# In TensorE's pinned order, which of two ready steps goes first ahead of a change of PSUM banks

## The chip, the core and the metric

The kernel runs on one core of a Trainium2 chip. The metric is the device time of one execution in microseconds. Three runs of the kernel before took 911.75, 911.88 and 913.54 us; the median is 911.88.

## The reference

Agent attention is followed by a two-layer network with a silu between. There are 2 batches of 12480 rows of 128 numbers, 49 agents, and 2048 hidden units. The input q, k and agents are drawn eight times larger than in the first lines of the reference's set-up.

```python
def sm(a, b):
    s = scale * (a @ b.transpose(0, 2, 1))
    s = s - s.max(-1, keepdims=True)
    e = np.exp(s)
    return e / (e.sum(-1, keepdims=True) + 1e-09)
a2k = sm(agents, k)
agent_v = a2k @ v
q2a = sm(q, agents)
x = (q2a @ agent_v).astype(np.float32)
h = x @ w_in
g = h * (1.0 / (1.0 + np.exp(-h)))
return (g @ w_out).astype(np.float32)
```

## The kernel before

The product of agent_v and w_in is formed once for each batch, as the tiles A2h and A2l (a high and a low half in 16 bits). So the first layer multiplies the turned softmax of q (the tile pT) by this product, with 64 rows of contraction, and two such matmuls stand side by side in the two halves of TensorE's rows.

The rows are cut into 26 pieces of 960 tokens, and the hidden units into 16 slices of 128. That gives 416 first-layer steps (`front`, line 574: six matmuls of 480 columns, three pairs, into the PSUM tile h) and 416 second-layer steps (`back`, line 616: twelve matmuls, six pairs, into the two PSUM banks of o). Between the two layers stand, for each slice, the silu on ScalarE (`gate`, line 594: g from h), and for each pair of slices the split of g into hi and lo (`split`): hi on ScalarE (line 606) or on VectorE (line 608), and lo on VectorE (line 612). After 16 second-layer steps a piece is done and goes out through os (lines 657 and 659). The work on q, k and v for later pieces and for the second batch (scores, transposes, sums) runs between these steps and uses TensorE's full array.

The second-layer steps go in fours, numbered r = 0 to 3. Each step uses both halves of TensorE's rows, and each half adds into one bank of o. After r = 1 the halves exchange their banks. The steps r = 1 and r = 2 read the same pair of slices. So that the two halves never add into one bank at a time, the matmuls of r = 2 wait for a token: GpSimd's memset (line 640) waits for the last matmuls of r = 1, and TensorE waits for the memset. This is the change of PSUM banks; there are 104 of them.

The order on every engine is made when the kernel is built, and pinned. A planner steps through time by its own table of durations, and at each instant every engine takes its next piece of work: `pe()` (line 1138) chooses for TensorE, `act()` for ScalarE and `dve()` for VectorE. In `pe()` background work that is due goes first; then a first-layer step, when a PSUM tile h is free (there are two) and its input is there; then a second-layer step, when its lo is there and, for r = 2, the token is set by the planner's reckoning (`told_end`); then other background work. `nf` and `nb` count the first- and second-layer steps that were placed. Whether ScalarE or VectorE makes a hi tile is chosen in `act()` and `dve()` by who is free, so it follows from when the steps stand.

Of the kernel before, what the change touches and what calls it, by code (L numbers as in the profile page):

```python
# [55 lines left out]
def agent_attention_then_silu_mlp(ctx, tc, qT, kT, vP, agT, w_in, w_outP, outT):  # L56
# [4 lines left out]
    NB = DFF // P  # L61
# [3 lines left out]
    NW = DFF // WW  # L65
# [37 lines left out]
    def warm(n):  # L103

        for _ in range(n):
            r = T.matmul(o1[:, GRP * NA:], ones12, ones12[:, 0:512 - GRP * NA], start=True, stop=True)
        warmed.append(1)
        return r
# [456 lines left out]
    NS = len(steps)  # L565
# [8 lines left out]
    def front(s):  # L574
        b, i, j = steps[s]
        t, w = pT[b, i], batch[b]
        ps = ph.tile([P, 2, 512], F32, tag="h", name=f"h{s}")
        fs = slice(j * P, (j + 1) * P)
        for n, (wt, x) in enumerate((("A2h", 0), ("A2l", 0), ("A2h", 1))):
            for u in range(2):  # L580
                rs = slice(u * RT, (u + 1) * RT)
                T.matmul(ps[:, u, :HT], w[wt][rs, fs], t[rs, x * HB:(x + 1) * HB, 0:CH],  # L582
                         start=(n == 0), stop=(n == 2))
        if j == NB - 1:
            pT.pop((b, i))
        if s % 2 == 0:
            hid[s // 2] = gg.tile([P, 2, 2, HT], F32, tag="g", name=f"g{s}", bufs=3)
        hps[s] = ps
# [27 lines left out]
    def back(k):  # L616


        m, r = divmod(k, 4)
        p = 2 * m + (0, 1, 1, 0)[r]  # L620
        turn = (m + r // 2) % 2
        b, i, j = steps[2 * p]
        hi, lo = hid[p]
        a, z = k % NB == 0, k % NB == NB - 1
        mms = {}
        if a:
            acc[0] = last_acc[0] = po.tile([P, HT], F32, tag="o0", name=f"o0_{k}")
            acc[1] = last_acc[1] = po.tile([P, HT], F32, tag="o1", name=f"o1_{k}")
        for x in range(2):
            for n, (wt, g) in enumerate(((woh, hi), (wol, hi), (woh, lo))):  # L630
                for t in range(2):
                    rs = slice(t * RT, (t + 1) * RT)
                    u = t ^ turn
                    mm = T.matmul(acc[u], wt[rs, j + x, :], g[rs, x, u, :],  # L634
                                  start=(a and x == 0 and n == 0), stop=(z and x == 1 and n == 2)).ins
                    mms[t] = mm
                    if r == 2 and x == n == 0:
                        tc.add_manual_dep(mm, acc["told"].name, SYNC, reason="banks")
        if r == 1:
            acc["told"] = G.memset(token, 0.0).ins  # L640
            for mm in mms.values():
                tc.add_manual_dep(acc["told"], mm.name, SYNC, reason="banks")
        if r > 1:
            hid.pop(p)
# [36 lines left out]
    def in_order():  # L681

        new = list(bb[mark[0]:])
        for i in new:
            if i.engine in prev:
                tc.add_manual_dep(i, prev[i.engine].name, ORDER, reason="order")
            prev[i.engine] = i
        mark[0] = len(bb)
# [22 lines left out]
    def free(r):  # L711
        n = len(used[r]) - have[r]
        return n < 0 or used[r][n] is not None and used[r][n] <= now

    def take(r):
        used[r].append(None)
        return len(used[r]) - 1
# [3 lines left out]
    def job(eng, us, fn, *args, **kw):  # L721
        j = Job(eng, us, fn, *args, **kw)
        bg[eng].append(j)
        return j
# [36 lines left out]
    def q_first(key, lt, t):  # L761
        l = first("S", QB, load, *key, take=("kq",), t=lt)
        w = "o1" if key[2] else "sc"
        x = first("P", 1.75, lambda key: q_scores32(key, o1 if key[2] else psum(512)), key, deps=[l], take=(w,),
                  give=("kq",), t=6 + t)
        x = first("D", 0.97, q_sub, key, deps=[x], take=("D",), give=(w,), t=9 + t)
        x = first("A", 0.52, q_exp, key, deps=[x], table="exp", t=9 + t)
        x = first("D", 1.3, q_norm, key, deps=[x], t=14 + t)
        x = first("D", 0.77, q_parts, key, deps=[x], give=("D",), t=14 + t)
        return first("S", TB, q_turn, key, deps=[x], take=("pT",), t=QT)  # L770

    keeps = {n: q_first(Q[n], (2.5, 6.5)[n], (0, 0)[n]) for n in range(NQ0)}
# [30 lines left out]
    for g, i0 in enumerate(range(0, NST, 2)):  # L803
# [21 lines left out]
        for u in range(n):  # L825
            i = i0 + u
            lv = first("S", VB, load, "v", 0, i, take=("vt0",), t=V_LOAD + i)
            w = "tp" if u else "sc"
# [37 lines left out]
    wdone = [job("D", 1.2, split_w_out, h, 1, deps=[whi[h], pieces[0, 0]], rel=FIRST, due=(2, 10)[h]) for h in range(NW)]  # L866
# [25 lines left out]
    for n in range(NQ0, len(Q), 1):  # L892
        q_jobs(n)
        if n % 2 or n == len(Q) - 1:
            m = len(exps)
# [9 lines left out]
    for g, i in enumerate(range(0, NST, K_EXP)):  # L905
# [4 lines left out]
        for u in range(n):  # L910
            key = ("k", b, i + u)
            r = max(0, s + K_STEP * u)
# [14 lines left out]
        for u in range(n):  # L927
            key = ("v", b, i + u)
            r = s + 3 + V_STEP * u
# [31 lines left out]
    LAT, DRAIN, TABLE, SAFE, HOLD = 0.06, 0.17, 1.28, 0.4, 0.5  # L961
    now = 0.0
    at = {e: 0.0 for e in "PDASG"}
    table = None
    nf, nb = 0, 0
    silu_end, lo_end, os_end, told_end = {}, {}, {}, {}
# [168 lines left out]

    mode = "row"

    def pe():
        nonlocal nf, nb, mode
        if bg_pe(lambda j: mode == "full" or nf >= j.due - 2 or nb % NB == 0 and not free("o")):  # L1140
            return True
        sw = 0.1 if mode == "full" else 0.0
        if nf < NS and free("h") and (nf % NB or keeps[nf // NB].end is not None and keeps[nf // NB].end + LAT <= now):
            b, i, j = steps[nf]
            x = pieces.get((b, j // PB))
            if (x is None or x.end is not None and x.end + LAT <= now) and (nf % 2 or free("g")):
                mine["h", nf] = take("h")
                if nf % 2 == 0:
                    mine["g", nf // 2] = take("g")
                front(nf)  # L1150
                in_order()
                at["P"] = now + 0.606 + sw
                mode = "row"
                silu_todo.append((at["P"] + DRAIN + LAT, nf))
                nf += 1
                if nf % NB == 0:
                    used["pT"][keeps[nf // NB - 1].has.pop("pT")] = at["P"] + DRAIN + LAT
                return True
        m, r = divmod(nb, 4)
        p = 2 * m + (0, 1, 1, 0)[r]  # L1160
        w = wdone[nb % NB // (NB // NW)]
        if nb < NS and lo_end.get(p, 1e9) + LAT <= now and (nb % NB or free("o")) and \
                (r != 2 or told_end[m] <= now) and w.end is not None and w.end + LAT <= now:
            if nb % NB == 0:
                take("o")
            back(nb)
            in_order()
            at["P"] = now + 1.212 + sw
            mode = "row"
            e = at["P"] + DRAIN + LAT  # L1170
            if r == 1:
                told_end[m] = e + 0.2
            if r > 1:
                used["hl"][mine["hl", p]] = e
            if nb % NB == NB - 1:
                os_todo.append([e, None, [], nb, 0.0])
            nb += 1
            return True
        if bg_pe(None):
            return True  # L1180
        if nf == 0 and not warmed:
            warm(WARM)
            in_order()
            at["P"] = now + 4.0
        elif nf == 0 and not st.get("open"):
            warm(2)
            in_order()
            at["P"] = now + 0.5
        else:
            return False  # L1190
        return True

    def bg_pe(only):
        nonlocal mode
        j = pick("P", only)
        if j:
            us = j.us + (0.1 if mode == "row" else 0.0)
            mode = "full"
            start(j, now, us)
        return j is not None  # L1200
# [14 lines left out]
    while nb < NS or os_todo or any(bg[e] for e in "PDASG"):  # L1215
        for e, fn in (("S", queue), ("P", pe), ("A", act), ("D", dve)):
            while at[e] <= now and fn():
                pass
        now = round(now + 0.02, 2)
        assert now < 2000, (nf, nb, free, [[(j.fn.__name__, j.args, j.rel) for j in bg[e]][:3] for e in bg])  # L1220
# [26 lines left out]
```

## Time and profile before

| what | us |
|---|---|
| median of three runs | 911.88 |
| span of the profiled execution | 912.4 |
| time around the span | not given by the page |
| TensorE busy | 887.7 |
| VectorE busy | 791.7 |
| ScalarE busy | 769.5 |
| GpSimd busy | 15.4 |

The span runs from the first to the last instruction of the profiled execution. Matmuls overlap with the one ahead, so their mean duration (0.36 us) is longer than the distance between two pairs (0.20 us). In the rows, "x2" stands for two instructions that follow each other, and square brackets hold idle time of the engine ahead of the row, and who ended it.

### The profile page before, as it was taken

Reading aid. Unit: us, or ns where it says so; the run is one execution under the profiler, and the core shown is the slowest. Engines: PE = TensorE matmul, PEld = TensorE weight load, DVE = VectorE, ACT = ScalarE, POOL = GpSimd, SP = SyncE. Lnnn points to the kernel's source line nnn. Section 1 sums busy time; section 2 is a strip of 40 time slices with the busy share of each in tenths; the row PEclk is TensorE's granted clock in tenths of the full one; section 3 lists DMA queues with packets and bytes.
Section 4 is the critical chain, followed back from the end, with each engine's and each line's share of the span. In section 5 each row is a group of like instructions: output and inputs, shape, how many; then the busy total and the mean of one; then the engine's idle time right before and its main releaser. Section 6 shows DMA issues by size and latency. Waiting matters only on the chain.

```text
span 912.4 us, 20334 instructions
## 1 busy us (share of the span) xinstructions
PE 887.7 (97%) x8879; PEld 442.0 (48%) x8879; DVE 791.7 (87%) x838; ACT 769.5 (84%) x729; POOL 15.4 (2%) x114
## 2 busy tenths in 40 slices
PE   8989899999999999999999999999999999999997
PEld 5554454444444454544445445444454454444443
DVE  5869989798899798899889899898998998988773
ACT  2669999999888799988889889889898898898783
POOL 1000000000000000000000000000000000000000
PEclk9999999999999999999999999999999999999999
DMA  8981123241232112211011111111201110101000
GB/s 311 410 231 56 54 58 110 78 120 40 82 99 78 51 49 72 72 34 55 24 35 38 40 53 37 39 41 34 56 28 51 35 56 26 31 14 35 22 23 22
DMA packets 43412, 63.91 MB, mean 70 GB/s; under 512 B 29475, under 2 KB 29731, under 8 KB 42811
## 3 DMA queue, kind: packets, MB, share of 16 engines
q1 hardware_dynamic: 43323, 62.61, 22.8%
q8 instruction: 69, 1.13, 0.5%
q14 instruction: 20, 0.16, 0.1%
HBM read 43.01 MB, written 12.78 MB: 61 GB/s over the span
## 4 chain that ended last, share of the span: by engine, by line
PE 85%; DVE 8%; DMA 3%; issue 2%; ACT 1%; POOL 1%; SPq 0%; POOLq 0%; DVEq 0%; ACTq 0%
PE o L634 52%; PE h L582 25%; DVE lo L612 3%; DMA k<-kT 2%; PE tp L450 1%; DMA vx<-vP 1%; DVE hi L608 1%; PE sc L434 1%; PE sc L351 1%; PE h_ps L351 1%; PE sc L332 1%; POOL token L640 1%; DVE mx L171 0%; PE o_ps L450 0%; PE sc L334 0%
## 5 line engine op out<-in xcount | busy, mean ns | idle before, releaser
L612 DVE SCALAR_TENSOR_TENSOR lo<-g,tS,hi 128x1920 f16<-128x1920 f32 x208 | 457.4, 2214 | 35.2 <-ACT hi L606 27.6
L594 ACT ACTIVATE g<-h,sA 128x960 f32<-128x960 f32 x416 | 422.1, 1060 | 65.4 <-PE h L582 62.7
L634 PE MATMUL o<-hi,woh 64*128 64x480 f16 x1664 | 307.3, 363 | 9.6 <-POOL token L640 8.9
L634 PE MATMUL o<-lo,woh 64*128 64x480 f16 x1664 | 306.7, 362 | 0.3 <-DVE lo L612 0.3
L634 PE MATMUL o<-hi,wol 64*128 64x480 f16 x1664 | 306.7, 362 | 0.0
L582 PE MATMUL h<-pT,A2h 64*128 64x480 f16 x1664 | 283.7, 363 | 1.9 <-ACT g L594 1.7
L634 PEld LDWEIGHTS <-woh 64*128 64x128 f16 x3328 | 167.1, 94 | 192.1 <-POOL token L640 21.7
L606 ACT ACTIVATE hi<-g,tS 128x1920 f16<-128x1920 f32 x116 | 220.1, 1898 | 15.8 <-PE o L634 14.6
L582 PE MATMUL h<-pT,A2l 64*128 64x480 f16 x832 | 153.2, 362 | 0.0
L582 PEld LDWEIGHTS <-A2h 64*128 64x128 f16 x1664 | 86.4, 94 | 101.2 <-issue 18.7
L634 PEld LDWEIGHTS <-wol 64*128 64x128 f16 x1664 | 83.3, 94 | 77.5
L608 DVE TENSOR_SCALAR hi<-g,tS 128x1920 f16<-128x1920 f32 x92 | 111.6, 1213 | 7.5 <-PE o L634 3.8
L582 PEld LDWEIGHTS <-A2l 64*128 64x128 f16 x832 | 41.5, 94 | 34.9 <-DVE A2l L522 0.3
L657 DVE TENSOR_SCALAR os<-o,oS 128x480 f32<-128x480 f32 x26 | 18.6, 717 | 39.3 <-PE o L634 39.2
L659 ACT ACTIVATE os<-o,oS 128x480 f32<-128x480 f32 x26 | 17.2, 662 | 18.5 <-PE o L634 18.3
L734 DVE SCALAR_TENSOR_TENSOR khl<-q,ik,khl 128x960 f16<-128x960 f32 x24 | 29.1, 1211 | 0.0
L731 ACT ACTIVATE khl<-q,ik 128x960 f16<-128x960 f32 x24 | 26.3, 1096 | 2.7 <-DVE ik L183 2.7
L640 POOL MEMSET token<- 1x1 f32 x104 | 12.8, 123 | 889.5 <-PE o L634 848.1
L171 DVE TENSOR_REDUCE mx<-q 128x1 bf16<-128x960 f32 x24 | 27.4, 1147 | 0.0
L594 ACT ACT_TABLE_LOAD x17 | 21.8, 1283 | 0.3
L351 PE MATMUL h_ps<-k,ag_all 128*64 128x480 f32 x52 | 16.7, 727 | 3.2 <-DMA k<-kT 3.1
L332 PEld LDWEIGHTS <-khl 128*128 128x128 f16 x192 | 14.8, 96 | 9.9 <-issue 8.1
(170 smaller groups left out, 507.9 us busy)
## 6 DMA issues: line engine op xcount, KB each, us to landing
k<-kT SPq DMA_DIRECT2D x26, 480.0 KB, 5.9
q<-qT SPq DMA_DIRECT2D x26, 480.0 KB, 4.3
outT<-os SPq DMA_DIRECT2D x25, 480.0 KB, 2.6
vt<-vP SPq DMA_DIRECT2D x13, 480.0 KB, 5.6
vt<-vP SPq DMA_DIRECT2D x9, 512.0 KB, 10.8
raw_in<-w_in SPq DMA_DIRECT2D x2, 1024.0 KB, 7.9
raw_out<-w_outP SPq DMA_DIRECT2D x2, 1024.0 KB, 9.9
vx<-vP SPq DMA_DIRECT2D x4, 512.0 KB, 10.2
```

Of the source, the lines that this page charges most:

```text
L171: V.tensor_reduce(mx[:n], x, axis=AX.X, op=ALU.max, apply_absolute_value=True)
L332: T.matmul(ps[:, c, :], hi[:, cs], ah, start=True, stop=False)
L351: T.matmul(ps[u * RT:(u + 1) * RT], ag_all[:, key[1], :], t[:, u * HT:(u + 1) * HT], start=True, stop=True)
L582: T.matmul(ps[:, u, :HT], w[wt][rs, fs], t[rs, x * HB:(x + 1) * HB, 0:CH], start=(n == 0), stop=(n == 2))
L594: A.activation(hid[s // 2][:, s % 2], hps.pop(s)[:, :, :HT], AF.Silu, scale=batch[b]["sA"][:, 0:1])
L606: A.activation(hid[p][1], g, AF.Copy, scale=t)
L608: V.tensor_scalar(hid[p][1], g, t, None, op0=ALU.mult)
L612: V.scalar_tensor_tensor(lo, g, t, hi, op0=ALU.mult, op1=ALU.subtract)
L634: mm = T.matmul(acc[u], wt[rs, j + x, :], g[rs, x, u, :], start=(a and x == 0 and n == 0), stop=(z and x == 1 and n == 2)).ins
L640: acc["told"] = G.memset(token, 0.0).ins
L731: A.activation(t[:, 0, 0:ST], tiles[key], AF.Copy, scale=st[key, "inv"][:, 0:1])
L734: V.scalar_tensor_tensor(l[:, 0:ST], tiles.pop(key), st.pop((key, "inv"))[:, 0:1], hi[:, 0:ST], op0=ALU.mult, op1=ALU.subtract)
```

## The change

A helper asks whether the next second-layer step could be placed now, by the same test that stands further down in `pe()`. When the next second-layer step is r = 1 (the last ahead of a change of banks) and could be placed, a first-layer step is not placed ahead of it.

```diff
+    def back_ready():
+        m, r = divmod(nb, 4)
+        p = 2 * m + (0, 1, 1, 0)[r]
+        w = wdone[nb % NB // (NB // NW)]
+        return nb < NS and lo_end.get(p, 1e9) + LAT <= now and (nb % NB or free("o")) and \
+            (r != 2 or told_end[m] <= now) and w.end is not None and w.end + LAT <= now
+
     def pe():
         nonlocal nf, nb, mode
         if bg_pe(lambda j: mode == "full" or nf >= j.due - 2 or nb % NB == 0 and not free("o")):
             return True
         sw = 0.1 if mode == "full" else 0.0
-        if nf < NS and free("h") and (nf % NB or keeps[nf // NB].end is not None and keeps[nf // NB].end + LAT <= now):
+        hold = nb % 4 == 1 and back_ready()
+        if not hold and nf < NS and free("h") and (nf % NB or keeps[nf // NB].end is not None and keeps[nf // NB].end + LAT <= now):
             b, i, j = steps[nf]
```

The order of TensorE at the 67th bank change (second-layer steps 265 and 266), in the kernel before. A step of line 634 reads hi or lo and one of the two weights woh and wol; "waits Pool_49" marks the matmul that waits for the token.

```order
L634 LDWEIGHTS wol
L634 MATMUL o_256_8093<-hi_8216,wol 128x480
L634 LDWEIGHTS woh
L634 MATMUL o_256_8092<-lo_8217,woh 128x480
L634 LDWEIGHTS woh
L634 MATMUL o_256_8093<-lo_8217,woh 128x480
L634 LDWEIGHTS woh [waits Pool_49]
L634 MATMUL o_256_8093<-hi_8216,woh 128x480
L634 LDWEIGHTS woh
L634 MATMUL o_256_8092<-hi_8216,woh 128x480
```

The same bank change on TensorE in the changed kernel: the end of step 265 and what follows it.

```order
L634 LDWEIGHTS woh
L634 MATMUL o_256_8081<-lo_8194,woh 128x480
L634 LDWEIGHTS woh
L634 MATMUL o_256_8082<-lo_8194,woh 128x480
L582 LDWEIGHTS A2h_5544
L582 MATMUL h_8309<-pT,A2h_5544 128x480 [waits Activation_49]
L582 LDWEIGHTS A2h_5544
L582 MATMUL h_8309<-pT,A2h_5544 128x480
```

And, twenty rows further on TensorE in the changed kernel, the start of step 266.

```order
L582 LDWEIGHTS A2h_5544
L582 MATMUL h_8316<-pT,A2h_5544 128x480
L582 LDWEIGHTS A2h_5544
L582 MATMUL h_8316<-pT,A2h_5544 128x480
L634 LDWEIGHTS woh [waits Pool_49]
L634 MATMUL o_256_8082<-hi_8193,woh 128x480
L634 LDWEIGHTS woh
L634 MATMUL o_256_8081<-hi_8193,woh 128x480
```

Before, the token's wait stands right behind the last matmul of step 265, and two first-layer steps stand ahead of that step; in the changed kernel the two first-layer steps stand between the last matmul of step 265 and the wait.

The order of ScalarE in the kernel before, ahead of and behind the 18th output step os (line 659): g is the silu (line 594), hi the high half (line 606), khl a split of q.

```order
L594 ACTIVATE g_8815<-h_8808,sA_5617 128x960
L594 ACTIVATE g_8815<-h_8819,sA_5617 128x960
L731 ACTIVATE khl_106<-q_8_8308,ik 128x960
L594 ACTIVATE g_8869<-h_8862,sA_5617 128x960
L594 ACTIVATE g_8869<-h_8871,sA_5617 128x960
L594 ACTIVATE g_8903<-h_8896,sA_5617 128x960
L659 ACTIVATE os_8924<-o_272_8524,oS_5620 128x480
L594 ACTIVATE g_8903<-h_8917,sA_5617 128x960
```

The order of ScalarE in the changed kernel, some rows ahead of the same output step.

```order
L606 ACTIVATE hi_8618<-g_8557,tS_5548 128x1920
L594 ACTIVATE g_8590<-h_8627,sA_5546 128x960
L594 ACTIVATE g_8642<-h_8635,sA_5546 128x960
L606 ACTIVATE hi_8665<-g_8590,tS_5548 128x1920
L594 ACTIVATE g_8642<-h_8658,sA_5546 128x960
L594 ACTIVATE g_8689<-h_8682,sA_5546 128x960
L606 ACTIVATE hi_8722<-g_8642,tS_5548 128x1920
L594 ACTIVATE g_8689<-h_8725,sA_5546 128x960
```

Between the 17th and the 18th output step ScalarE has six rows of line 606 in the changed kernel and four before, and a hi now stands between the two silus of the following pair; over the whole program line 606 stands 145 times on ScalarE (116 before) and line 608 stands 63 times on VectorE (92 before).

## Rows read from the trace of the kernel before

**Rows 1.** the page, part 1 (busy time) and the clock row of part 2

```profile
PE 887.7 (97%) x8879; PEld 442.0 (48%) x8879; DVE 791.7 (87%) x838; ACT 769.5 (84%) x729; POOL 15.4 (2%) x114
...
PEclk9999999999999999999999999999999999999999
```

**Rows 2.** the page, part 4: the chain of waits by line

```profile
PE o L634 52%; PE h L582 25%; DVE lo L612 3%; DMA k<-kT 2%; PE tp L450 1%; DMA vx<-vP 1%; DVE hi L608 1%; PE sc L434 1%; PE sc L351 1%; PE h_ps L351 1%; PE sc L332 1%; POOL token L640 1%; DVE mx L171 0%; PE o_ps L450 0%; PE sc L334 0%
```

**Rows 3.** waits of TensorE: who waited for whom, us in total, times, longest

```profile
PE o L634 <- POOL token L640: 8.9, 30, 0.6
...
PE h L582 <- ACT g L594: 1.7, 3, 1.4
...
PE o L634 <- DVE lo L612: 0.3, 1, 0.3
```

**Rows 4.** timeline (start, us, what) of a bank change with nothing between

```profile
579.34 0.39 PE L634 MATMUL o<-hi,wol 64*128 64x480 f16 x2
...
579.54 0.39 PE L634 MATMUL o<-lo,woh 64*128 64x480 f16 x2
580.05 0.09 POOL L640 MEMSET token<- 1x1 f32 x1 [7.58 <-PE o L634]
...
580.20 0.38 PE L634 MATMUL o<-hi,woh 64*128 64x480 f16 x2 [0.27 <-POOL token L640]
```

**Rows 5.** timeline of a bank change with one first-layer step between

```profile
571.89 0.37 PE L634 MATMUL o<-lo,woh 64*128 64x480 f16 x2
...
572.38 0.09 POOL L640 MEMSET token<- 1x1 f32 x1 [7.65 <-PE o L634]
...
572.70 0.37 PE L634 MATMUL o<-hi,woh 64*128 64x480 f16 x2
```

**Rows 6.** timeline of a bank change with one short matmul between

```profile
395.97 0.38 PE L634 MATMUL o<-hi,woh 64*128 64x480 f16 x2 [0.16 <-POOL token L640]
```

**Rows 7.** timeline of a late token: DVE, GpSimd, TensorE

```profile
470.58 1.22 DVE L608 TENSOR_SCALAR hi<-g,tS 128x1920 f16<-128x1920 f32 x1 [0.19 <-ACT g L594]
...
470.79 1.04 POOL L640 MEMSET token<- 1x1 f32 x1 [7.20 <-PE o L634]
470.90 0.37 PE L582 MATMUL h<-pT,A2h 64*128 64x480 f16 x2
...
471.89 0.38 PE L634 MATMUL o<-hi,woh 64*128 64x480 f16 x2 [0.62 <-POOL token L640]
```

**Rows 8.** all instructions of line 640: ns min, median, max

```profile
L640 POOL MEMSET token<- x104: 88/88/1047, 73.6 to 905.4; 1x1 f32 x104
```

**Rows 9.** timeline of a full-array group between second-layer steps

```profile
533.04 0.37 PE L634 MATMUL o<-lo,woh 64*128 64x480 f16 x2
533.34 0.20 PE L332 MATMUL sc<-agh,khl 128*128 128x49 f16 x1
...
533.93 0.18 PE L334 MATMUL sc<-agh,khl 128*128 128x49 f16 x1
534.04 0.38 PE L634 MATMUL o<-hi,woh 64*128 64x480 f16 x2
```

**Rows 10.** the page, part 5: the costliest groups that the change meets

```profile
L612 DVE SCALAR_TENSOR_TENSOR lo<-g,tS,hi 128x1920 f16<-128x1920 f32 x208 | 457.4, 2214 | 35.2 <-ACT hi L606 27.6
L594 ACT ACTIVATE g<-h,sA 128x960 f32<-128x960 f32 x416 | 422.1, 1060 | 65.4 <-PE h L582 62.7
...
L606 ACT ACTIVATE hi<-g,tS 128x1920 f16<-128x1920 f32 x116 | 220.1, 1898 | 15.8 <-PE o L634 14.6
...
L608 DVE TENSOR_SCALAR hi<-g,tS 128x1920 f16<-128x1920 f32 x92 | 111.6, 1213 | 7.5 <-PE o L634 3.8
```

**Rows 11.** busy time by stretch: PE, PEld, DVE, ACT, POOL

```profile
607.00:884.00 277.00, 272.88 (x2772) 133.66 (x2770) 245.83 (x218) 238.01 (x215) 5.10 (x36) 1.00 0.12 34
```

**Rows 12.** ScalarE by line from 607 to 884: busy, mean, idle before

```profile
L594 ACT ACTIVATE g<-h,sA 128x960 f32<-128x960 f32 x145 | 147.1, 1059 | 29.9 <-PE h L582 29.5
L606 ACT ACTIVATE hi<-g,tS 128x1920 f16<-128x1920 f32 x38 | 72.2, 1899 | 8.4 <-PE o L634 8.0
```

## The prediction

> **What bounds the kernel now.** The busy row of the page comes first: TensorE works 887.7 of 912.4 us, VectorE 791.7, ScalarE 769.5, and the clock row shows full clock in every slice [rows 1]. The chain of waits says the same by line: 77% of the span is the two matmul lines, 52% for the second layer (line 634) and 25% for the first (line 582); GpSimd's token has 1% [rows 2]. So what is left to win stands in TensorE's own idle time, and the third view, its waits, names it: 30 times it waits for the token of line 640, 8.9 us together, and behind that come only 1.7 us for silu (three waits) and 0.3 us for one lo [rows 3].
>
> A token wait is idle time after the matmul before has ended, and pairs of matmuls normally overlap, so the loss is read from starts. Pairs follow each other every 0.20 us (579.34, 579.54). At a bank change with nothing between, the next pair starts at 580.20, 0.66 us after 579.54: 0.46 us lost [rows 4]. With one first-layer step between, the token is set at 572.38 and the second-layer step starts in its turn at 572.70; since 0.15 us from the token's start to the next pair is enough (580.05 to 580.20), 0.17 us is to spare [rows 4, 5]. With a single short matmul between, 0.16 us of idle time stays [rows 6]. A third kind is dearer: at 470.79 the token's memset takes 1.04 us, and the step that had a first-layer step ahead of it starts at 471.89 where 471.10 was its turn [rows 7]. Counted along the order, the 30 waits are 24 bare changes, 3 with a short matmul and 3 late tokens; 24 x 0.27 + 3 x 0.16 + 3 x 0.62 is 8.8, which is the row.
>
> **The change part by part.** It adds no instruction and removes none from TensorE; it alters which of two ready steps goes first at every fourth second-layer step, and all later choices follow from that.
>
> Bare changes. In the order of the changed kernel 10 of the 104 bank changes have nothing between them, where 24 have now; 51 have exactly two first-layer steps and 23 exactly one (31 and 25 now). 14 x 0.46 = 6.4 us, all of it on TensorE's own path. Changes with only one short matmul go from three to two: 0.2 us.
>
> Groups of full-array work. Entering one costs 0.10 us (533.04 to 533.34 instead of 0.20) and leaving it 0.09 us (533.93 to 534.04, where its 24 matmuls otherwise follow at 0.02 to 0.03) [rows 9]. The order has 72 such groups between steps, now 78: 6 x 0.19 = 1.1 us.
>
> The step that is held. It runs 1.21 us later (six pairs at 0.20), but TensorE is not idle meanwhile; its silu, and through that hi and lo, come later. That is paid only if a later step has to wait. ScalarE hides it: it idles 29.9 us ahead of silus in the stretch 607 to 884 [rows 12]. If that cover is gone, TensorE waits for h or lo.
>
> Who scales. In the new order ScalarE makes 145 of the hi tiles and VectorE 63, now 116 and 92. ScalarE gains 29 x 1.90 = 55 us of work (to 825), VectorE loses 29 x 1.21 = 35 us (to 757) [rows 1, 10]. Both still lie beside TensorE's 888 us over the whole; the stretch of the rival below is the tight one.
>
> New waits. The second-layer steps now follow their data more closely. Along the order, with steps of 0.61 and 1.21 us, the step ahead of a bank change starts a median of 15.9 us after the last first-layer step of its pair, and 12.6 us at the tenth percentile; in the new order 11.4 and 7.3. What must fit in is silu, hi and lo, 1.06 + 1.90 + 2.21 = 5.2 us, plus queueing [rows 10]. No row shows these waits. From below: the present 1.7 + 0.3 us vanish too, -2.0. From above: each of the 14 changes that were mended waits as long for lo as it did for the token, +6.4. I take +1.0, near the lower end, since today's greedy order shows only 2.0 us of such waits in 912 [rows 3].
>
> Late tokens. The long memset ends at 471.83, right behind VectorE's hi (line 608, 470.58 to 471.80), and the longest of the 104 is 1047 ns where the median is 88 [rows 7, 8]. So a token that falls due inside a line 608 is set when that ends. Three such now cost 3 x 0.79 = 2.4 us. If they fall by chance, 63 x 1.21 us of 912 is 8% of the time, and a mean remainder of 0.6 us gives 10 x 0.08 x 0.6 = 0.5 for the bare changes, 23 x 0.08 x 0.44 = 0.8 for those with one step (0.17 spare) and 51 x 0.08 x 0.07 = 0.3 with two (0.78 spare): 1.6 us. I count the difference as nothing; the ends are -2.4 (none) and +6.0 (rival).
>
> By the Trainium skill, page "SBUF — State Buffer", section "Who interferes with whom", VectorE and GpSimd share one pair of SBUF ports as an exclusive lock that a tensor_scalar can take for its whole length, while an operation with two SBUF inputs hinders only GpSimd's reads. The trace agrees at 1.04 us [rows 7]; by that rule the line 608s alone matter and the sum stands, whereas if line 612, 457 of the 912 us, blocked too, about half of the tokens would be late, and the 88 ns median says that they are not [rows 8, 10].
>
> DMA. SyncE's queue has as many rows as before with some output stores and loads exchanged; tiles are loaded many steps ahead, and no transfer stands in TensorE's waits after the opening. I count nothing; with that cover gone, the step that reads the tile waits, and this lies inside the upper bound of the new waits.
>
> Sum: -6.4 - 0.2 - 1.1 + 1.0 = -6.7 us. The page gives the profiled execution's span, 912.4, and no time around it; the runs' median is 911.88, half a microsecond below, so the sum goes on that: 905.2 us.
>
> **The rivals.**
> ScalarE takes over (slower). Between the output steps at 607 and 884 (the nine blocks from k = 256) the new order gives ScalarE 53 hi tiles for 38. 238.0 + 15 x 1.90 = 266.5 us of work in 277 [rows 11, 12]. Today it also idles 29.9 + 8.4 us there, nearly all for TensorE. If half of that idling stays, because silu must wait for steps that are now held, the stretch takes 285.7, 8.7 more; against it stand the 7 bare changes saved elsewhere, 3.2. Time 917. It decides from 10.5 us of idling upward. For it: hi now often stands between the two silus of a pair. Against: a late ScalarE finds its h ready and does not idle.
>
> The wait only changes its name. The step pulled forward waits for lo instead of token: the +6.4 above replaces +1.0, so -1.3, 910.6 us. For it: 7.3 us against 5.2. Against: two such waits of any size in the present trace.
>
> Late tokens take the gain. Orders repeat, so a phase can lock: one late token in every second block of 16 steps, 13 more of 0.46 to 0.79, is +6 to +10; at +6 the time is 911.2. For it: a filler of one step spares only 0.17 us. Against: there are 29 fewer line 608s.
>
> That the change does nothing is excluded by the order (24 to 10).
>
> **How the numbers follow.** Forecast 0.77, ScalarE 0.07, renamed wait 0.09, late tokens 0.05, something not listed 0.02. About 0.2%, 1.8 us, is what a measurement tells from no change: faster is below 910.1, slower above 913.7. Faster takes the forecast and a third of the two middle rivals, 0.82; same 0.11; slower 0.07. The forecast's own ends are -6.7 - 3.0 (waits at -2.0) for 902.2 and, with half the upper bound of new waits (3.2), 907.4; the range reaches a little toward the renamed wait: 902.5 to 909.5.
>
> **What would show it.** TensorE's token waits fall from 30 to about 14 and from 8.9 us to under 5; its span less its busy time shrinks; waits for g and lo together stay under 4 us; lines 606 and 608 count 145 and 63, with ScalarE near 825 us busy. Wrong would be: more than 5 us of TensorE waiting for lo or g, ScalarE without idle time from 607 on, or more than six memsets near 1 us.

## The result, and the profile after

The changed kernel takes 904.43 us (median of six runs, 904.13 to 905.79) against 912.12 us for the kernel before on the same chips; the ratio is 0.9912 (95% interval 0.9899 to 0.9924), so 7 to 9 us are gained. The prediction was 905.2 us.

The spans of the two profiled executions, 912.4 and 902.4, differ by more. The reason is the opening, which both programs carry out in the same order. The rows of line 634 show when the first second-layer step starts and when the last pairs start; first the kernel before, then the changed one.

```profile
L634 PE MATMUL o<-hi,woh x1664: 359/362/373, 69.3 to 907.4; 64*128 64x480 f16 x185
```

```profile
L634 PE MATMUL o<-hi,woh x1664: 359/363/374, 66.8 to 897.3; 64*128 64x480 f16 x185
```

From 69.3 to 907.4 are 838.1 us, from 66.8 to 897.3 are 830.5: 7.6 us less, which is the gain of the medians. This stretch is used below for every kernel, since the opening alone varies by 2.8 us between profiled executions (66.8 to 69.6).

The page after, busy time and the chain by engine, answers to [rows 1, 2].

```profile
PE 878.9 (97%) x8879; PEld 450.0 (50%) x8879; DVE 759.8 (84%) x809; ACT 819.1 (91%) x758; POOL 13.9 (2%) x114
...
PE 77%; DVE 9%; ACT 6%; DMA 4%; issue 3%; SPq 0%; POOL 0%; POOLq 0%; ACTq 0%; DVEq 0%
```

TensorE still has 97%, but ScalarE has risen from 84 to 91%, and the chain now runs 15% of the span over VectorE and ScalarE. The waits of TensorE after, against [rows 3]:

```profile
PE o L634 <- POOL token L640: 3.5, 12, 0.8
PE h L582 <- ACT g L594: 3.3, 6, 1.4
PE o L634 <- DVE lo L612: 2.4, 4, 1.1
```

Token waits fell from 30 to 12 and from 8.9 to 3.5 us; waits for silu and lo rose from 2.0 to 5.7 us. In both kernels 1.56 us of these stand in the opening, ahead of the first second-layer step; so behind it they rose from 0.45 to 4.2 us. The larger of the two, in the kernel before:

```profile
67.73 0.38 PE L582 MATMUL h<-pT,A2h 64*128 64x480 f16 x2 [1.40 <-ACT g L594]
```

The groups of the page show who works more, against [rows 10]:

```profile
L612 DVE SCALAR_TENSOR_TENSOR lo<-g,tS,hi 128x1920 f16<-128x1920 f32 x208 | 459.5, 2215 | 88.7 <-ACT hi L606 83.8
L594 ACT ACTIVATE g<-h,sA 128x960 f32<-128x960 f32 x416 | 421.8, 1058 | 33.7 <-PE h L582 29.6
...
L606 ACT ACTIVATE hi<-g,tS 128x1920 f16<-128x1920 f32 x145 | 275.2, 1899 | 2.1
...
L608 DVE TENSOR_SCALAR hi<-g,tS 128x1920 f16<-128x1920 f32 x63 | 76.5, 1214 | 6.0 <-ACT g L594 5.2
```

ScalarE's idle time ahead of silus has halved (65.4 to 33.7 us), and VectorE now stands 84 us ahead of lo waiting for ScalarE's hi (28 before). The 67th bank change, which was bare like the one of [rows 4], is now filled; timeline of TensorE and GpSimd in the changed kernel:

```profile
615.96 0.36 PE L634 MATMUL o<-lo,woh 64*128 64x480 f16 x2
...
616.46 0.09 POOL L640 MEMSET token<- 1x1 f32 x1 [5.38 <-PE o L634]
616.57 0.57 PE L582 MATMUL h<-pT,A2h 64*128 64x480 f16 x4
...
617.18 0.37 PE L582 MATMUL h<-pT,A2h 64*128 64x480 f16 x2
...
617.38 0.37 PE L634 MATMUL o<-hi,woh 64*128 64x480 f16 x2
```

The token is set at 616.55, and the second-layer step starts at 617.38 in its turn, 0.20 us after the pair ahead of it.

**The account.** For every step of both traces, the distance from its first matmul to that of the next step, less its own length (0.608 or 1.215 us), is time beyond the steps. It sums to 83.9 us before and 76.4 after. By what stands in it:

| time beyond the steps, us | before | after | difference | predicted |
|---|---|---|---|---|
| bare bank changes (24, 10) | 10.85 | 4.90 | -5.95 | -6.4 |
| tokens waited for inside groups | 0.97 | 0.64 | -0.33 | -0.2 |
| late tokens behind a first-layer step (3, 0) | 2.35 | 0 | -2.35 | 0 |
| full-array groups without waits | 62.13 | 61.49 | -0.64 | -1.1 |
| waits for silu and lo | 1.09 | 6.30 | +5.21 | +1.0 |
| waits for the output step os | 1.29 | 0 | -1.29 | 0 |
| the rest: waits inside groups, small differences | 5.26 | 3.08 | -2.18 | 0 |
| sum | 83.9 | 76.4 | -7.5 | -6.7 |

A wait counts here with the time that it puts a step behind its turn, 0.16 us more than the idle time in a row of waits. The waits for silu and lo include four for silu that are too short for the list of waits (one before and three after, 0.06 to 0.13 us of idle time). Of the -2.18 us of the rest, 1.5 us are waits of full-array groups for their own inputs.

### The profile page after: what moved, and what is told of

The parts are those of the page before. It is cut to its first block, busy times and chain, and to the rows that moved or that the text cites. A ratio compares the mean times of both kernels' runs of the same rounds, so it can differ in the third digit from the quotient of the medians.

```text
span 902.4 us, 20267 instructions
## 1 busy us (share of the span) xinstructions
PE 878.9 (97%) x8879; PEld 450.0 (50%) x8879; DVE 759.8 (84%) x809; ACT 819.1 (91%) x758; POOL 13.9 (2%) x114
## 4 chain that ended last, share of the span: by engine, by line
PE 77%; DVE 9%; ACT 6%; DMA 4%; issue 3%; SPq 0%; POOL 0%; POOLq 0%; ACTq 0%; DVEq 0%
PE o L634 46%; PE h L582 23%; DVE lo L612 5%; ACT g L594 4%; DMA k<-kT 2%; PE tp L450 1%; DMA vx<-vP 1%; DVE hi L608 1%; PE sc L434 1%; PE sc L351 1%; ACT hi L606 1%; DVE khl L734 1%; PE sc L332 1%; ACT L594 1%; DVE mx L171 0%
## 5 line engine op out<-in xcount | busy, mean ns | idle before, releaser
L594 ACT ACTIVATE g<-h,sA 128x960 f32<-128x960 f32 x416 | 421.8, 1058 | 33.7 <-PE h L582 29.6
L582 PE MATMUL h<-pT,A2h 64*128 64x480 f16 x1664 | 287.1, 363 | 3.6 <-ACT g L594 3.3
L606 ACT ACTIVATE hi<-g,tS 128x1920 f16<-128x1920 f32 x145 | 275.2, 1899 | 2.1
L634 PEld LDWEIGHTS <-woh 64*128 64x128 f16 x3328 | 170.4, 94 | 178.2 <-POOL token L640 8.5
L634 PEld LDWEIGHTS <-wol 64*128 64x128 f16 x1664 | 85.2, 94 | 79.0
L608 DVE TENSOR_SCALAR hi<-g,tS 128x1920 f16<-128x1920 f32 x63 | 76.5, 1214 | 6.0 <-ACT g L594 5.2
L582 PEld LDWEIGHTS <-A2l 64*128 64x128 f16 x832 | 42.6, 94 | 33.7 <-DVE A2l L522 0.3
L657 DVE TENSOR_SCALAR os<-o,oS 128x480 f32<-128x480 f32 x26 | 18.6, 714 | 13.0 <-PE o L634 12.8
L659 ACT ACTIVATE os<-o,oS 128x480 f32<-128x480 f32 x26 | 17.2, 663 | 12.4 <-PE o L634 12.4
L332 PE MATMUL sc<-agh,khl 128*128 128x49 f16 x192 | 17.2, 185 | 0.6 <-DVE D L534 0.6
```

What stands on the lines that cost most here:

```text
L332: T.matmul(ps[:, c, :], hi[:, cs], ah, start=True, stop=False)
L594: A.activation(hid[s // 2][:, s % 2], hps.pop(s)[:, :, :HT], AF.Silu, scale=batch[b]["sA"][:, 0:1])
L606: A.activation(hid[p][1], g, AF.Copy, scale=t)
L608: V.tensor_scalar(hid[p][1], g, t, None, op0=ALU.mult)
L634: mm = T.matmul(acc[u], wt[rs, j + x, :], g[rs, x, u, :], start=(a and x == 0 and n == 0), stop=(z and x == 1 and n == 2)).ins
L657: V.tensor_scalar(o[:, 0:HT], last_acc[0], oS, None, op0=ALU.mult)
```

## The experiments

All times are medians beside 912.0 to 912.3 us for the kernel before on the same chip, with the ratio and its 95% interval. Single executions of the kernel before lie up to 3 us apart, so where a run differs by about 1 us, its rows say more than its median. "By the account" means the sums of time beyond the steps, made for that run's own trace as in the table above.

**Control: the hold at another place.**

```diff
-        hold = nb % 4 == 1 and back_ready()
+        hold = nb % 4 == 3 and back_ready()
```

> Control: the same hold, but ahead of r = 3, where no banks change. In its order 28 bank changes are bare (24 before, 10 in the change), 5 have one short matmul (3), TensorE has 72 full-array groups (78), and ScalarE makes 149 of the hi tiles (116). Filled-bank-change theory: +4 x 0.46 + 2 x 0.23 - 6 x 0.19 = +1.2 us, 913.3 us, and no gain. Rival 'the gain comes from hi tiles moved from VectorE to ScalarE' (29 moved for -7.7 us in the change, 33 here): 903 to 905 us. Rival 'it comes from fewer full-array groups' (72 here as in the change): 904 to 905 us.

Measured: 911.2 us, ratio 0.9984 (0.9975 to 0.9992); stretch 837.4 us. Both rivals fall: neither as many hi tiles on ScalarE nor as few groups bring the gain. But the time is 1.1 us lower, not 1.2 higher. The bare changes cost what they should (28 for 12.4 us), and the late tokens of before are gone from TensorE's path. Its waits on TensorE:

```profile
PE o L634 <- POOL token L640: 8.4, 33, 0.3
...
PE tp L176 <- DVE mx L171: 2.4, 3, 0.8
...
PE h L582 <- ACT g L594: 1.6, 2, 1.4
```

The longest token wait is 0.3 us, where it was 0.6. Memsets still meet line 608 (the longest takes 1035 ns), but other work of TensorE covers them. By the account 2.35 us of late tokens and 1.3 us of a wait for D are gone, while the three waits for mx cost 2.9 us (one, of 0.5 us, before) and the bare changes 1.5 us more; the groups, os and smaller terms make up the rest. So the late tokens count as a term of their own in the account; this run does not separate them from the other terms.

**Half of the hold.**

```diff
-        hold = nb % 4 == 1 and back_ready()
+        hold = nb < 208 and nb % 4 == 1 and back_ready()     # first_half
+        hold = nb >= 208 and nb % 4 == 1 and back_ready()    # second_half
```

> The hold only for second-layer steps 0 to 207. 18 bare bank changes (24 before, 10 in the change), 2 short (3), 72 groups (78), 132 hi tiles on ScalarE. Filled-bank-change theory: -6 x 0.46 - 0.2 - 1.1 + 0.5 of new waits = -3.6 us, 908.5 us. Rival 'hi tiles': 16 of 29 moved, 907.9 us. Rival 'groups': all six gone, 904.4 us.

> The hold only from second-layer step 208 on. 14 bare bank changes (24 before, 10 in the change), 4 short (3), 73 groups (78), 139 hi tiles on ScalarE. Filled-bank-change theory: -10 x 0.46 + 0.2 - 1.0 + 0.5 = -4.9 us, and up to 2 us more if the three late tokens go, which all lie in this half: 905.2 to 907.2 us. Rival 'hi tiles': 23 of 29 moved, 906.0 us. Rival 'groups': 905.7 us.

Measured: 906.14 us, ratio 0.9931 (0.9916 to 0.9945), and 908.84 us, 0.9958 (0.9945 to 0.9971); stretches 832.1 and 834.9. The first half brings more than the bare changes in it, the second less, and they do not follow the hi tiles or the groups either; both expected times by the theory of filled changes (908.5, and 905.2 to 907.2) were missed as well. By the account of the two runs, the hold in the first half gains 3.5 us up to step 208: four bare changes (1.95 us), one late token (0.8 us) and 2.8 us of waits inside groups and for os are gone, and 2.1 us of waits for lo are new. Another 2.6 us come behind step 208, where the hold no longer acts but the altered order goes on: two bare changes (1.0 us), five groups fewer (0.9 us) and smaller terms. The hold in the second half takes ten bare changes (4.5 us), two late tokens (1.6 us) and five groups (1.0 us) away, and gets 2.5 us of waits for silu and 0.9 for lo. One of the three late tokens, that of [rows 7], stands ahead of step 186, so they do not all lie in the second half, as the expectation has it. The waits of TensorE with the hold in the first half only:

```profile
PE o L634 <- POOL token L640: 6.4, 22, 0.6
...
PE o L634 <- DVE lo L612: 2.1, 3, 1.1
PE h L582 <- ACT g L594: 1.8, 3, 1.4
```

**More of the same: the hold ahead of r = 0 too.**

```diff
-        hold = nb % 4 == 1 and back_ready()
+        hold = nb % 4 < 2 and back_ready()
```

> The hold ahead of r = 0 too, so that the two second-layer steps ahead of a bank change both go before a first-layer step. 7 bare bank changes (10 in the change), 3 short (2), 74 groups (72), 150 hi tiles on ScalarE (145), 60 changes with exactly two first-layer steps (51). Filled-bank-change theory: -3 x 0.46 + 0.2 + 0.4 = -0.8 us against the change, 903.6 us, if no more waits for lo and silu come in. Rival 'the step that is pulled forward waits for its data instead': 906 us or more, with TensorE's waits for lo and g above the 5.7 us that they have in the change.

Measured: 923.55 us, ratio 1.0117 (1.0103 to 1.0131); stretch 849.5. The rival holds, and by far more than it asked. Waits of TensorE:

```profile
PE h L582 <- ACT g L594: 12.8, 32, 1.4
PE o L634 <- DVE lo L612: 6.3, 13, 1.3
...
PE o L634 <- POOL token L640: 2.1, 8, 0.3
```

The token has almost gone (2.1 us), and 19.1 us of waits for data stand in its place. ScalarE has 150 hi tiles, five more than in the change, and idles 44.9 us ahead of silus:

```profile
L594 ACT ACTIVATE g<-h,sA 128x960 f32<-128x960 f32 x416 | 419.9, 1058 | 44.9 <-PE h L582 43.9
```

So ScalarE is not full, it waits for h while TensorE waits for it. That the data is asked for too early fits this; no run separates it from the longer holding back of the first-layer steps.

**A longer token, in both kernels.**

```diff
-    token = cp.tile([1, 1], F32, name="token")
+    token = cp.tile([1, 128], F32, name="token")
```

> The kernel before with a token of 128 numbers instead of one, so that the memset takes longer by some D, which its rows tell (0.1 to 0.3 us by the memsets of other sizes on the page). The order is that of the kernel before. Theory that a bare change stands on the path with its whole length: 27 x D (24 bare, 3 short) and, for D over 0.17 us, 25 x (D - 0.17) for those with one first-layer step. With D = 0.2: +5.4 + 0.8 = +6.2 us, 918.5 us. Rival 'the path runs through ScalarE and VectorE, and TensorE's wait only fills their lead': +1 us or less.

> The change with a token of 128 numbers. Theory that a bare change stands on the path: 12 x D (10 bare, 2 short) and 23 x (D - 0.17) where D is over 0.17 us. With D = 0.2: +2.4 + 0.7 = +3.1 us, half of what the same token costs the kernel before. Rival 'ScalarE bounds the changed kernel': no more than +1 us, since it has lead to make up.

The memset takes 107 ns longer (before, then after):

```profile
L640 POOL MEMSET token<- x104: 195/195/1154, 71.6 to 906.1; 1x128 f32 x104
```

```profile
L640 POOL MEMSET token<- x104: 195/195/1213, 71.7 to 897.8; 1x128 f32 x104
```

Measured: 915.13 us, ratio 1.0026 (1.0017 to 1.0036), and 907.73 us, 0.9942 (0.9929 to 0.9954). With D = 0.107 the theory gives 27 x D = 2.9 us and 12 x D = 1.3 us. The stretch grows from 838.1 to 841.0 (+2.9) and from 830.5 to 832.5 (+2.0); in the second, 1.3 us are bare changes and tokens inside groups, and 0.95 us is one token that met a line 608 in this run. By the medians the changed kernel loses more, 2.7 us (0.9942 against 0.9912, each to about 0.0013), so the stretch, not the time, tells the two sums apart; the rival's bound of 1 us is passed by either. A bare change is on the path with its whole length, in the changed kernel too, although ScalarE is busier there.

**Late tokens: three attempts.** First, VectorE may not begin a hi while a token is due.

```diff
-                and not lows:
+                and not lows and not (nb % 4 == 2 and told_end.get(nb // 4, 0.0) > now):
```

> The kernel before, but VectorE may not begin a hi tile (line 608) while a token is due. Its order keeps what the change moved elsewhere: 23 bare bank changes (24), 1 short (3), 77 groups (78), hi tiles 114 and 94 (116 and 92). Theory that the late tokens are a cost of their own: 3 x 0.79 = 2.4 us go, with 0.46 + 0.46 + 0.19 from the order: 3.5 us, ratio about 0.996. Rival 'only bare changes count': -1.1 us, ratio 0.999.

Measured: 910.62 us, ratio 0.9985 (0.9976 to 0.9994); stretch 836.5. The edit missed its aim, probably because line 608 and the token stand differently in the planner's time than on the chip: the longest memset is still 1046 ns, and token waits are 8.7 us in 28, of which four are late tokens (3.0 us by the account). So this says nothing of late tokens; the 1.4 us come from other places in the order.

Second, two tiles by name.

```diff
-                and not lows:
+                and not lows and hi_todo[0][1] not in (194, 202):
```

> The kernel before, in which two hi tiles (pairs 194 and 202) are kept off VectorE: those whose line 608 ran while the tokens at 847.8 and 878.2 us were due. TensorE's order is that of the kernel before up to about 845 us; in all, 23 bare bank changes (24), 78 groups as before, hi tiles 118 and 90. Theory 'a late token costs TensorE 0.79 us': -2 x 0.79 - 0.46 = -2.0 us, ratio 0.9978; from the first second-layer step to the end 841.1 us against 843.15. Rival 'only bare changes count': -0.5 us, ratio 0.9995, 842.7 us.

Measured: 911.41 us, ratio 0.9988 (0.9978 to 0.9998); stretch 836.8, 1.3 us less. The stretch lies between the two, and the interval of the ratio holds both 0.9978 and 0.9995, so the time decides nothing; the rows do. Token waits:

```profile
PE o L634 <- POOL token L640: 7.4, 27, 0.6
```

They fell by 1.5 us in three waits, so both late tokens and one bare change are gone as expected (2 x 0.62 + 0.27 of idle time); a new wait for silu (0.4 us) and 0.3 us more for os took some of it back.

Third, all three tiles, which alters the order from 470 us on.

```diff
+                and not lows and hi_todo[0][1] not in (96, 194, 202):
```

> As the run with two hi tiles moved, and pair 96 too (the late token at 470.8 us). That alters every choice after about 470 us, with no hold in the kernel: 16 bare bank changes (24 before, 10 in the change), 3 short (3), 73 groups (78), 47 changes with exactly one first-layer step (25), hi tiles 136 and 72. Theory 'bare changes and late tokens count, whatever fills them': -8 x 0.46 - 3 x 0.79 - 0.5 = -6.6 us less 2 us or so of new waits: 905.5 to 908 us, ratio 0.993 to 0.995. Rival 'the gain needs the hold's place in the order': 911 us or more.

Measured: 907.53 us, ratio 0.9951 (0.9936 to 0.9966); stretch 833.6, 4.5 us less. Inside the expectation, in a kernel without the hold. Its token waits:

```profile
PE o L634 <- POOL token L640: 4.9, 19, 0.3
```

Eight of its memsets still take 0.46 to 0.61 us, but no token wait is longer than 0.3 us, so that steps ahead of the wait cover them. By the account eight bare changes (3.6 us), the late tokens (2.35 us) and five groups (0.75 us) are gone, against 0.7 us of new waits for silu and os and 1.5 us of small differences. The gain doesn't take the hold; it takes filled bank changes and tokens that are not late.

**More hi tiles on ScalarE, with the hold.**

```diff
-HI_WAIT = 0.6
+HI_WAIT = 1.3
```

> The change with HI_WAIT 1.3 for 0.6, so that VectorE takes a hi tile only if ScalarE is busy for longer: hi tiles 169 and 39 (145 and 63 in the change), 5 bare bank changes (10), 2 short (2), 69 groups (72), 26 with one first-layer step (23). Theory 'bare changes only': -5 x 0.46 - 0.4 = -2.7 us against the change, 901.7 us. Rival 'ScalarE takes over': its work grows by 24 x 1.90 = 46 us to 865 us, TensorE's waits for g go from 3.3 to 9 us or more, and the time is 906 us or above.

Measured: 920.52 us, ratio 1.0082 (1.0069 to 1.0094); stretch 845.4. Busy time, then waits of TensorE:

```profile
PE 885.8 (96%) x8879; PEld 459.9 (50%) x8879; DVE 732.2 (80%) x785; ACT 859.5 (94%) x782; POOL 15.7 (2%) x114
```

```profile
PE h L582 <- ACT g L594: 10.1, 20, 1.4
PE o L634 <- DVE lo L612: 5.5, 7, 2.7
PE o L634 <- DVE os L657: 3.0, 9, 0.8
```

ScalarE has taken over, with the fewest bare changes but one: 18.6 us of waits for g, lo and os against 2.2 for tokens.

**A version that beats both.** The change, with the guard of the first attempt and VectorE more willing to take a hi.

```diff
-HI_WAIT = 0.6
+HI_WAIT = 0.0
-                and not lows:
+                and not lows and not (nb % 4 == 2 and told_end.get(nb // 4, 0.0) > now):
```

> The change, with line 608 kept off a due token, and VectorE taking a hi tile as soon as ScalarE is busy (HI_WAIT 0.0 for 0.6). 2 bare bank changes (10 in the change), 3 short (2), 61 with two first-layer steps (51), 74 groups (72), hi tiles 142 and 66. Theory that bare changes, late tokens and waits for g and lo add up: -8 x 0.45 - 0.5 + 0.2 + 0.4 = -3.5 us against the change if the waits for g and lo stay at 5.7 us: 901 us, ratio 0.988. Rival 'data comes too late': each filled change draws a wait of its own, 904 us or more, and the waits for g and lo go above 9 us.

Measured: 902.05 us (901.5 to 902.11), ratio 0.9882 (0.9868 to 0.9895); stretch 827.8. Waits of TensorE:

```profile
PE h L582 <- ACT g L594: 3.0, 7, 1.4
PE o L634 <- POOL token L640: 2.5, 8, 0.5
...
PE o L634 <- DVE lo L612: 0.7, 2, 0.5
```

Tokens 2.5 us and data 3.7 us (1.56 of them in the opening): the fill is kept, and the waits for data are below those of the change (5.7). The guard misses its aim here too: 14 memsets are held up by a line 608, the longest for 1007 ns, and by the account three late tokens cost 2.0 us, while the two bare changes that are left cost 0.9. So the gain over the change (-2.7 us in the stretch) comes from eight bare changes fewer (-4.0 us) and from shorter waits for data. Which of its two edits does this was not tried apart.

## Why the prediction was right

The direction and the mechanism held. That the sum of -6.7 us came so close to -7.6 is luck in part: new waits were forecast 4.2 us too low, and three terms that stood at nothing in the sum (late tokens, waits for os, the rest) brought 5.8 us.

- Bare changes: right. -6.4 predicted, -5.95 in the account. Nine of the ten that are left cost 0.44 us; one met a line 608 and cost 0.95. The long token shows that this time stands on the path in both kernels.
- New waits: the term that was mis-sized most, +1.0 predicted, +5.2 measured, near its upper bound of +6.4. Half of the growth is lo (0.5 to 3.1 us), half silu (0.6 to 3.2 us), while the upper bound was worked out from lo alone. I took the term from the two rows of waits in the kernel before, and read them wrongly: 1.56 of their 2.0 us stand in the opening and stay in every run, so they neither could vanish (the lower end of -2.0) nor say much of the stretch that the change alters. The distance along the order pointed the right way. It was to fall from 12.6 to 7.3 us at the tenth percentile, with 5.2 us needed; in the traces it fell from 13.2 to 7.9. Rows of an order that is being altered tell little of the waits in the next one.
- One such wait shows how they arise. In the changed kernel ScalarE's hi stands between two silus, and the next first-layer step needs the PSUM tile h that the second one reads:

```profile
810.19 1.89 ACT L606 ACTIVATE hi<-g,tS 128x1920 f16<-128x1920 f32 x1
...
811.99 1.04 ACT L594 ACTIVATE g<-h,sA 128x960 f32<-128x960 f32 x1
812.10 0.36 PE L634 MATMUL o<-lo,woh 64*128 64x480 f16 x2
...
813.09 0.38 PE L582 MATMUL h<-pT,A2h 64*128 64x480 f16 x2 [0.62 <-ACT g L594]
```

- Late tokens: counted at nothing, -2.35 in the account (the lower end was -2.4). By chance 1.6 us of them should have stayed; none stayed behind a first-layer step, and one raised a bare change by 0.5 us. The longest memset fell from 1047 to 745 ns:

```profile
L640 POOL MEMSET token<- x104: 88/88/745, 71.1 to 895.3; 1x1 f32 x104
```

  Fewer line 608s are not the reason: five memsets were held up by one before, and seven are now, with 63 of them instead of 92. They were held up for a shorter time, or had more steps ahead of the wait to cover them; the prediction did not foresee this, so this part of the gain is luck. That a late token costs time is seen in rows, but the run that took two of them away gave back part of it.
- Groups: -1.1 predicted, -0.64 measured without their waits. The waits inside groups and those for os fell by another 1.5 and 1.3 us, which I had not counted.
- The rival of ScalarE: not reached, but not far. The piece of the program that the prediction named, between the 16th and the 25th output step, now lies from 600.05 to 872.41; busy time by engine there, and ScalarE's lines:

```profile
600.05:872.41 272.36, 269.71 (x2756) 142.94 (x2753) 227.30 (x201) 262.02 (x228) 3.33 (x36) 1.00 0.13 36
```

```profile
L594 ACT ACTIVATE g<-h,sA 128x960 f32<-128x960 f32 x143 | 144.8, 1059 | 8.5 <-PE h L582 8.3
L606 ACT ACTIVATE hi<-g,tS 128x1920 f16<-128x1920 f32 x53 | 100.6, 1901 | 0.9
```

  It takes 272.4 us for 277 before. ScalarE works 96% of it (fourth engine of the first row; 266.5 us of work were forecast), and its idle time ahead of silus fell from 29.9 [rows 12] to under 9 us: a late ScalarE did not idle, as the prediction had it. The run with 24 more hi tiles crossed the line.

- The renamed wait: true in part. Waits for data took back 5.2 us of 12.7 us gained; with the hold at two steps they took back more than all.

Of the marks that the prediction set, the tokens (12 waits, 3.5 us), the hi counts (145 and 63), ScalarE (819 us) and the memsets came out. The span less busy time hardly shrank (24.7 to 23.5 us), since the busy time itself fell by 8.8 us with the same 8879 matmuls. The waits for g and lo (5.7 us, opening included) went over the 4 us that were allowed, and over the 5 us that were to count as wrong. So the size of the new waits is the step that failed, and other terms made up for it.

## What to carry to other kernels

When an engine's order is pinned, a wait is removed by placing work behind the instruction that starts it, and this first term of the gain is the number of bare waits times the loss between starts, not the idle time in a row. Then count how much closer each consumer now follows its producer, step by step along the new order: the waits for data grow from there, and here a hold that went one step further lost more than the first had won. A relay by a small instruction on another engine has to be watched for what blocks that engine: here it is the place of the token and not the number of blocking instructions that decided.

## What the runs showed of the hardware that was not expected

A memset of one number on GpSimd takes 88 ns, of 128 numbers in one partition 195 ns, and either takes up to 1.05 or 1.21 us where VectorE's line 608 runs as it falls due [rows 7]. In the changed kernel such a late token stands at a bare bank change:

```profile
550.00 1.22 DVE L608 TENSOR_SCALAR hi<-g,tS 128x1920 f16<-128x1920 f32 x1
...
550.65 0.60 POOL L640 MEMSET token<- 1x1 f32 x1 [8.62 <-PE o L634]
...
551.30 0.38 PE L634 MATMUL o<-hi,woh 64*128 64x480 f16 x2 [0.79 <-POOL token L640]
```

The memset ends at 551.25, 0.03 us after line 608. All five memsets that a line 608 held up in the kernel before, and all seven in the changed one, end 0.03 us after it. Silus that follow each other on ScalarE start 0.94 to 0.96 us apart, though each lasts 1.06 us by its row.
